# Attention in seven tiles of 128 keys for two pairs of heads, instead of eight tiles of 112

## The chip, the cores and the metric

The kernel runs on one core of a Trainium2 chip. The metric is the device time of one execution in microseconds (us); the kernel before takes 1037.21 us (median of three runs, 1036.66 to 1038.28). A core has a matrix engine (TensorE, in the profile PE for its matmuls and PEld for the loading of their stationary operand), a vector engine (VectorE, DVE), an activation engine (ScalarE, ACT), GpSimd (POOL) and SyncE (SP, which here only starts DMA transfers). Each engine works through its own instructions in order; semaphores tie them together. TensorE writes to PSUM, which the kernel uses as four slots of 128 partitions by two banks of 512 floats.

## The reference

Three stages follow each other: an attention with a sigmoid in place of a softmax, a mixture of experts in which each token goes to one of eight experts, and a gated feed-forward layer.

```
B, H, S, HD = 4, 12, 448, 64                       # attention: q, k, v are (B, H, S, HD)
scores = q @ k.T / sqrt(HD) - log(S)
x = (sigmoid(scores) @ v)  -> (B * S, H * HD) = (1792, 768)
logits = normalised(x) @ normalised(expert_emb).T / tau ; e = argmax(logits) ; gate = softmax(logits)[e]
x = gate * (relu(x @ w1[e]) @ w2[e])               # w1: 768 x 1024, w2: 1024 x 768, 8 experts
out = (sigmoid(x @ w_gate) * (x @ w_val)) @ w_out  # 768 x 1536, 1536 x 768
```

The change is in the attention, and in the small pieces of the routing that run between its steps.

## The kernel before

The 48 heads are 24 pairs (`NP`). A pair fills 128 partitions, one head in partitions 0 to 63, the other in 64 to 127 (`kq`: the pair's keys, 448 columns, then its queries, 448 columns). The 448 keys are cut into `NCH` = 4 tiles of `CP` = 112. One tile of one pair is a unit, with three parts:

- `qk_unit` (L349 to L359): the transposed scores, 112 keys by 448 queries for either head, into one PSUM slot (a bank for each head). Keys and queries are split into a rounded part `hi` and a remainder `lo` (`split_pair`, L341: two VectorE instructions for a pair), and three matmuls hi·hi, hi·lo, lo·hi are summed (L358). The two heads stand in different halves of the array's rows. One ScalarE instruction (L359) then applies the sigmoid to both heads, 112 x 896 elements, into `attn`.
- `av_unit` (L361 to L369): `attn` times the values, in full float32, so that the profile shows two TensorE instructions for each matmul (L364). The contraction is over the tile's 112 keys. The two heads fill different halves of the array's columns. The four tiles of a pair are summed in one PSUM slot `av`; after the last, VectorE copies it to `xT` (L368).
- `logits_unit` (L373): the finished pair's part of the expert logits (L378), in the free bank of the next pair's `av` slot.

The step loop (L834 to L912) sets the order on all engines: it is written out by hand, and each engine's queue follows it. Step `g` makes the scores of units 2g and 2g+1, then the values of the two units before them. 48 steps do the 96 units, and one more step the last values. Other work is put between the steps by their number: `split_pair` two pairs ahead; `load_pair` (three buffers, refilled when a pair has been split) and `load_v` (four buffers) on SP's queue; the decoding of nine packed weight tiles on VectorE (`DEC_AT` says in which steps it begins; three instructions in three steps); after each batch of six pairs the turning of `xT` into rows (`rows_unit`, L402, six transposes on TensorE, a copy on ScalarE, a store to `xd` in DRAM by POOL's queue).

`G0` = 38 is the step after the third of the four batches; `q` counts from there. At `q` = 0 `choose` finds each token's expert (VectorE), at 2 `count` counts the tokens of each expert (TensorE, L477 to L482), then come `fullest`, `ranks` and others (VectorE), at 6 `first_ids` (TensorE, L552) and `gather(0)`, which fetches 128 token rows from `xd` by an indirect DMA on POOL's queue (L794), and at 8 `front(0)`, which transposes the fetched rows (L803). The last four `rows_unit` of the three batches stand at `q` = 0 to 3, so the last rows are stored to `xd` before `gather(0)` reads them.

Of the kernel before, what the change touches and what calls it, by code (L numbers as in the profile page):

```python
# [10 lines left out]
F32 = mybir.dt.float32  # L11
# [15 lines left out]
P = 128  # L27
CP = 112
NCH = S // CP
NPR = H // 2  # L30
NT = N // CP
NTC = N // P
# [18 lines left out]
NDEC = KF2 + NWO  # L51
DEC_ATT = 9
DEC_LEAD = 3
DEC_AT = (4, 8, 13, 17, 22, 26, 31, 36, 42)
DEC_MOE = 2

PZ = 10
# [48 lines left out]
def routed_kernel(ctx: ExitStack, tc: tile.TileContext, kqP, vP, emb, tau, w1P, w2P, wffP, cst, out):  # L106
# [11 lines left out]
    def slot(name):  # L118
        return psp.tile([P, 2, 512], F32, tag="ps", name=name)
# [149 lines left out]

    def load_pair(i):  # L270

        t = ap2.tile([P, 2 * S], F32, tag="kq", name=f"kq{i}", bufs=3)
        SP.dma_start(t, kqP[divmod(i, NPR)])
        kq_t[i] = t

    def load_v(i):
        v = ap2.tile([CP, NCH, P], F32, tag="v", name=f"v{i}", bufs=4)
        SP.dma_start(v.rearrange("p c d -> p (c d)"), vP[divmod(i, NPR)])
        v_t[i] = v

    tau_sb = cpool.tile([P, 1], F32, name="tau_sb")
    emb_sb = ap2.tile([E, D], F32, tag="xr", name="emb_sb", bufs=3)
# [25 lines left out]
    def prepare_constants():  # L308
        V.reciprocal(tau_sb, tau_sb)
        V.tensor_copy(upper_h, C("upper", CP))  # L310
        V.tensor_copy(iota_h, C("iota"))
        V.tensor_copy(ids_h, C("ids", CP))
        V.memset(ones_h, 1.0)
        G.memset(en, 0.0)
        sq = ap1.tile([E, D], BF16, tag="junk", name="sq")
        ssq = cpool.tile([E, 1], F32, name="ssq")
        A.activation(sq, emb_sb, AF.Square, accum_out=ssq)
        rt = cpool.tile([E, 1], F32, name="rt")
        G.tensor_tensor(out=rt, in0=ssq, in1=half_s[:E], op=ALU.pow)
# [17 lines left out]
    ss = cpool.tile([CP, NT], F32, name="ss")  # L337
    ssp = cpool.tile([CP, NCH, 3], F32, name="ssp")
    xT, split_t, attn_t, pav_t = {}, {}, {}, {}

    def split_pair(i):  # L341

        t = kq_t.pop(i)
# [5 lines left out]
    def qk_unit(i, c):  # L349

        hi, lo = split_t[i]
        at_ = ap2.tile([CP, 2, S], F32, tag="attn", name=f"attn{i}_{c}", bufs=6)
        attn_t[i, c] = at_
        ps = slot(f"sc{i}_{c}")
        for a, (k, q) in enumerate(((hi, hi), (hi, lo), (lo, hi))):
            for j in range(2):
                own = slice(j * HD, (j + 1) * HD)
                T.matmul(ps[:CP, j, :S], k[own, c * CP : (c + 1) * CP], q[own, S:], start=(a == 0), stop=(a == 2))  # L358
        A.activation(at_, ps[:CP, :, :S], AF.Sigmoid, bias=bias_s[:CP], scale=1.0 / math.sqrt(HD))  # L359

    def av_unit(i, c):  # L361
        v = v_t[i]
        for j in range(2):
            T.matmul(pav_t[i][j * HD : (j + 1) * HD, 0, :S], v[:, c, j * HD : (j + 1) * HD],  # L364
                     attn_t[i, c][:, j, :], start=(c == 0), stop=(c == NCH - 1))
        if c == NCH - 1:
            x = ap2.tile([P, S], F32, tag="xT", name=f"xT{i}", bufs=8)
            V.tensor_copy(x, pav_t.pop(i)[:, 0, :S])  # L368
            xT[i] = x  # L369
# [46 lines left out]
    def rows_part(part, c):  # L416

        t = TE + c
        k0, n = ((0, 3), (3, 2))[part]
        ps = slot(f"xr{t}_{part}")  # L420
        pv = ps[:CP, 0, : n * P]
        for k in range(n):
            T.transpose(pv[:, k * P : (k + 1) * P], xT[TE // NCH * NPR + k0 + k][:, c * CP : (c + 1) * CP], ident)
        x = ap2.tile([CP, D], F32, tag="xr", name=f"xr_sb{t}_{part}", bufs=3)[:, : n * P]
        A.copy(x, pv)
        (SP if part else G).dma_start(xd[t * CP : (t + 1) * CP, k0 * P : (k0 + n) * P], x)
        later = lambda: square(x, ssp[:, c, part : part + 1], f"{t}_{part}")
        if part and c >= 2:
            squares.append(later)
        else:  # L430
            later()
# [392 lines left out]
    SP.dma_start(emb_sb, emb)  # L824
    load_pair(2)
    load_v(1)
    load_v(2)
    AHEAD = 2
    for n in range(AHEAD):
        split_pair(n)  # L830
        load_pair(n + 3)

    G0 = 2 * NPR * (B - 1) + 2
    for g in range(2 * NP + 1):  # L834
        i, hh = divmod(g, 2)
        if i < NP:
            qk_unit(i, 2 * hh)
            qk_unit(i, 2 * hh + 1)
        if g == 2:
            prepare_constants()  # L840
        elif g == 3:
            prepare_directions()
        elif g == 4:
            prepare_experts()
        q = g - G0
        if g == 2 * NP:
            split_next(eng=G, hi_eng=V)
        ia, ha = divmod(g - 1, 2)
        if q == 2:
            count(0, TE)  # L850
        elif q == 6:
            first_ids(0, TE)
            gather(0)
        elif q == 8:
            front(0)
        if hh == 1 and i + AHEAD < NP:
            split_pair(i + AHEAD)
            if i + AHEAD + 3 < NP:
                load_pair(i + AHEAD + 3)
        if g >= 1:  # L860
            if ha == 0:
                pav_t[ia] = slot(f"av{ia}")
                if ia:
                    logits_unit(ia - 1)
            for c in range(2):
                av_unit(ia, 2 * ha + c)
            if ha == 0 and ia:
                logits_sum(ia - 1)
# [6 lines left out]
        if hh == 1 and i + 3 < NP:  # L875
            load_v(i + 3)
        b, c = divmod(g - 2 * NPR - 2, 2 * NPR)
        if 0 <= b < B - 1:
            if c == 0:
                logits_turn(b)  # L880
            if c < NCH:
                rows_unit(b, c)
        c = g - 2 * (NP - 3) - 2
        if 0 <= c < NCH:
            rows_part(0, c)
        if g >= 2 * NP - 1:
            for c in range(2):
                rows_part(1, 2 * (g - 2 * NP + 1) + c)
        if g == 2 * NP:
            logits_turn(B - 1)  # L890
        if q == 0:
            choose(0, TE)
            RED(out=ohf, in_=oh[:, :TE].rearrange("p t e -> p e t"), axis=AX.X, op=ALU.add)
            V.tensor_copy(ohs, ohf)
            V.tensor_copy(oh4, bct(ohf, NCH))
        elif q == 2:
            fullest()
            expert[0] = SP.value_load(es["tile"], min_val=0, max_val=E - 1)
            ranks(0, TE)
            fullest_ids(0, TE)  # L900
            first_tiles(0, TE)
        elif q == 3:
            columns(0, TE // 2)
        elif q == 4:
            columns(TE // 2, TE)
        if 4 <= q < 4 + NW1:
            load(order.index(("w1", 0, q - 4)))
        if q == 7:
            for k in (0, 1):
                load(order.index(("w2", 0, k)))  # L910
        if q in (6, 7, 8):
            split_next(hi_eng=V if q == 7 else None)  # L912

    hp_t = {}

# [496 lines left out]
```

## Time and profile before

| what | value |
|---|---|
| device time, median of three | 1037.21 us |
| the profiled execution's own time | 1037.45 us |
| its span, first to last instruction | 1035.6 us |
| TensorE busy, matmuls | 1006.4 us, 97% of the span |
| VectorE, ScalarE, GpSimd busy | 58%, 49%, 13% |
| mean granted TensorE clock | 0.99 |
| attention: first score to last value matmul | 4.9 us to about 175 us |

The attention is the first sixth of the span. In the page's 40 slices of 25.9 us each it is the first seven. A busy share is an average: what a change in one stage is worth is read from that stage's own rows. Matmuls are pipelined, so the start of one to the start of the next on the same part of the array tells their cost; the length of one alone holds the time that its last column needs to come out.

### The profile page before, as it was taken

The page shows a single profiled execution, that of the slowest core. Times are in us where ns is not written, and L with a number is a line of the kernel's source. Part 1 is how long each engine was busy: PE and PEld are TensorE (multiplying, and loading weights), DVE is VectorE, ACT ScalarE, POOL GpSimd, SP SyncE. Part 2 cuts the span into 40 slices and gives each one's busy share as a digit, 9 for nine tenths or more (in the row PEclk, how much of TensorE's full clock was granted, in tenths as well). Part 3 has the DMA queues.
Part 4 walks back from the last instruction along what each step waited for, and adds up shares of the span by engine and source line. Part 5 has one row for each costly group of instructions (what it writes and reads, how often), then busy time and mean ns, then how long its engine had stood idle before and what let it go on. Part 6 is the DMA issues. An engine that isn't in the chain of part 4 may idle for free.

```text
span 1035.6 us, 15304 instructions
## 1 busy us (share of the span) xinstructions
PE 1006.4 (97%) x6144; PEld 822.7 (79%) x6144; DVE 597.2 (58%) x660; ACT 503.1 (49%) x546; POOL 138.4 (13%) x109
## 2 busy tenths in 40 slices
PE   9999999878999999999999999999999999999996
PEld 4455455676887788888888899888899888899995
DVE  5665577986887877787658743334332333323551
ACT  5576678536766676777502432233322333323540
POOL 0010012643242122111100000200000000001001
PEclk9999999989999999999999999999999999999998
DMA  7878786112689876765458652422333333324630
GB/s 254 303 257 300 247 304 231 71 32 110 247 265 415 289 263 269 253 221 211 166 169 280 236 180 99 143 99 92 122 122 123 125 108 103 122 92 143 196 119 31
DMA packets 38526, 191.94 MB, mean 185 GB/s; under 512 B 4952, under 2 KB 5992, under 8 KB 36016
## 3 DMA queue, kind: packets, MB, share of 16 engines
q1 hardware_dynamic: 30560, 152.84, 43.3%
q0 software_dynamic: 7888, 38.05, 9.8%
q8 instruction: 50, 0.82, 0.3%
q14 instruction: 28, 0.23, 0.1%
HBM read 197.46 MB, written 31.16 MB: 221 GB/s over the span
## 4 chain that ended last, share of the span: by engine, by line
PE 73%; DVE 0%; issue 0%; DMA 0%; POOLq 0%; ACT 0%
PE gv L1154 11%; PE gv L1153 11%; PE gv L1155 11%; PE h L935 8%; PE o L921 5%; PE o L919 5%; PE o L920 5%; PE y L919 3%; PE y L921 3%; PE y L920 3%; PE qh L1024 1%; PE qy L1047 1%; PE hTp L954 1%; PE yTp L1139 1%; PE xTp L803 1%
## 5 line engine op out<-in xcount | busy, mean ns | idle before, releaser
L213 DVE TENSOR_TENSOR lo<-rawb,hi 128x1536 fp32r<-128x1536 f32 x173 | 302.1, 1756 | 289.9 <-ACT hi L212 286.3
L212 ACT CAST hi<-rawb 128x1536 fp32r<-128x1536 f32 x178 | 262.8, 1480 | 244.7 <-PE gv L1154 96.3
L1153 PE MATMUL gv<-yT,hi 128*128 128x512 f32 (+1 forms) x576 | 208.9, 363 | 0.0
L1155 PE MATMUL gv<-yT,lo 128*128 128x512 f32 (+1 forms) x576 | 208.9, 363 | 0.0
L1154 PE MATMUL gv<-yT,hi 128*128 128x512 f32 (+1 forms) x576 | 208.8, 363 | 0.0
L1155 PEld LDWEIGHTS gv<-yT,lo 128*128 128x128 f32 x576 | 108.7, 189 | 16.9
L1153 PEld LDWEIGHTS gv<-yT,hi 128*128 128x128 f32 x576 | 108.7, 189 | 16.8
L1154 PEld LDWEIGHTS gv<-yT,hi 128*128 128x128 f32 x576 | 108.7, 189 | 16.7
L919 PE MATMUL o<-hi,gh 128*128 128x384 f32 x336 | 112.8, 336 | 0.0
L921 PE MATMUL o<-lo,gh 128*128 128x384 f32 x336 | 112.3, 334 | 0.0
L920 PE MATMUL o<-hi,gl 128*128 128x384 f32 x336 | 112.3, 334 | 0.0
L359 ACT ACTIVATE attn<-sc,bias_s 112x896 f32<-112x896 f32 x96 | 91.2, 1001 | 41.9 <-PE sc L358 41.9
L1324 ACT CAST gh<-sg 128x512 fp32r<-128x512 f32 (+1 forms) x48 | 27.2, 567 | 132.1 <-DVE sg L1323 132.1
L364 PE MATMUL av<-attn,v 112*64 112x448 f32 x384 | 82.8, 552 | 0.0
L919 PE MATMUL y<-hi,hh 128*128 128x384 f32 x208 | 72.7, 349 | 0.0
L935 PE MATMUL h<-hi,xh 128*128 128x512 f32 x168 | 69.2, 412 | 3.5 <-PEq L1078 3.4
L935 PE MATMUL h<-lo,xh 128*128 128x512 f32 x168 | 67.1, 399 | 4.5 <-DVE lo L213 4.5
L921 PE MATMUL y<-lo,hh 128*128 128x384 f32 x208 | 70.5, 339 | 0.3 <-DVE lo L213 0.3
L920 PE MATMUL y<-hi,hl 128*128 128x384 f32 x208 | 70.3, 338 | 0.0
L1343 POOL DMA_INDIRECT out<-ob,idc x13 | 17.8, 1373 | 370.5 <-DVE ob L1372 340.1
L920 PEld LDWEIGHTS o<-hi,gl 128*128 128x128 f32 x336 | 63.1, 188 | 0.1
L919 PEld LDWEIGHTS o<-hi,gh 128*128 128x128 f32 x336 | 63.1, 188 | 0.1
(302 smaller groups left out, 1311.9 us busy)
## 6 DMA issues: line engine op xcount, KB each, us to landing
rawb<-wd SPq DMA_DIRECT2D x65, 768.0 KB
rawb<-in_w1P SPq DMA_DIRECT2D x52, 768.0 KB
rawb<-in_w2P SPq DMA_DIRECT2D x52, 768.0 KB
rawb<-in_wffP SPq DMA_DIRECT2D x16, 1536.0 KB
wd<-rawb POOLq DMA_DIRECT2D x16, 768.0 KB, 7.9
kq<-in_kqP SPq DMA_DIRECT2D x24, 448.0 KB
v<-in_vP SPq DMA_DIRECT2D x24, 224.0 KB
xd<-xr_sb POOLq DMA_DIRECT2D x12, 336.0 KB, 5.2
```

What stands on the lines that cost most here:

```text
L212: (hi_eng.tensor_copy if hi_eng else A.copy)(hi, raw)
L213: eng.tensor_sub(lo, raw, hi)
L359: A.activation(at_, ps[:CP, :, :S], AF.Sigmoid, bias=bias_s[:CP], scale=1.0 / math.sqrt(HD))
L364: T.matmul(pav_t[i][j * HD : (j + 1) * HD, 0, :S], v[:, c, j * HD : (j + 1) * HD], attn_t[i, c][:, j, :], start=(c == 0), stop=(c == NCH - 1))
L919: T.matmul(o, ah[:, ks], bh[:, w], start=(k == 0), stop=False)
L920: T.matmul(o, al[:, ks], bh[:, w], start=False, stop=False)
L921: T.matmul(o, ah[:, ks], bl[:, w], start=False, stop=(k == nk - 1))
L935: T.matmul(ps[:, half, :], x[:, k * P : (k + 1) * P], w[:, s * 512 : (s + 1) * 512], start=(k == 0 and x is xh and w is hi), stop=(k == KD ...
L1153: T.matmul(o, hi[:, a, k, :], yh[:, k, :n], start=(k == 0), stop=False)
L1154: T.matmul(o, hi[:, a, k, :], yl[:, k, :n], start=False, stop=False)
L1155: T.matmul(o, lo[:, a, k, :], yh[:, k, :n], start=False, stop=(k == KD - 1))
L1324: A.copy(gh[:, f, :n], sg[:, :n])
```

## The change

Two pairs of heads now share seven tiles of 128 keys (`NU` = 7). Of each pair, keys 0 to 383 are three whole tiles. The last 64 keys of both pairs make the joint tile, number 3 of the seven: pair 2d in rows 0 to 63, pair 2d+1 in rows 64 to 127. 12 doubles of pairs by 7 make 84 units in 42 steps. In the joint unit `qk_unit` does one float32 matmul for each head and pair, straight from `kq` without the split, and `av_unit` four matmuls of 64 rows by 64 columns, into the `av` slots of both pairs. So `kq` has to stay until the joint unit has read it (five buffers instead of three), and is loaded two pairs at a time after the joint unit; the values of two pairs are one load of 448 KB (two buffers), laid out on the host. The pieces of the routing and of the decoding get new step numbers, and `G0` becomes 33.

```diff
+NU = 2 * S // P
+KQ = 5
-DEC_AT = (4, 8, 13, 17, 22, 26, 31, 36, 42)
+DEC_AT = (3, 7, 11, 15, 19, 23, 27, 31, 36)
     def load_pair(i):
-        t = ap2.tile([P, 2 * S], F32, tag="kq", name=f"kq{i}", bufs=3)
+        t = ap2.tile([P, 2 * S], F32, tag="kq", name=f"kq{i}", bufs=KQ)
-    def load_v(i):
-        v = ap2.tile([CP, NCH, P], F32, tag="v", name=f"v{i}", bufs=4)
+    def load_v(d):
+        v = ap2.tile([P, NU, P], F32, tag="v", name=f"v{d}", bufs=2)
...
+    def parts_of(u):
+        d, n = divmod(u, NU)
+        if n == NU // 2:
+            return [(2 * d + p, S - HD, slice(p * HD, (p + 1) * HD)) for p in range(2)]
+        return [(2 * d + n // 4, n % 4 * P, slice(0, P))]
+    def qk_unit(u):
+        at_ = ap2.tile([P, 2, S], F32, tag="attn", name=f"attn{u}", bufs=6)
+        attn_t[u] = at_
+        ps = slot(f"sc{u}")
+        both = len(parts_of(u)) == 2
+        for a in range(1 if both else 3):
             for j in range(2):
                 own = slice(j * HD, (j + 1) * HD)
-                T.matmul(ps[:CP, j, :S], k[own, c * CP : (c + 1) * CP], q[own, S:], start=(a == 0), stop=(a == 2))
-        A.activation(at_, ps[:CP, :, :S], AF.Sigmoid, bias=bias_s[:CP], scale=1.0 / math.sqrt(HD))
+                for i, k0, rows in parts_of(u):
+                    hi, lo = (kq_t[i],) * 2 if both else split_t[i]
+                    k, q = ((hi, hi), (hi, lo), (lo, hi))[a]
+                    T.matmul(ps[rows, j, :S], k[own, k0 : k0 + rows.stop - rows.start], q[own, S:],
+                             start=(a == 0), stop=(both or a == 2))
+        A.activation(at_, ps[:, :, :S], AF.Sigmoid, bias=bias_s, scale=1.0 / math.sqrt(HD))
+    def first_unit(i):
+        return i // 2 * NU + i % 2 * (NU // 2)
+    def last_unit(i):
+        return first_unit(i) + NU // 2
+    def av_unit(u):
+        av_open(u)
+        v, at_ = v_t[u // NU], attn_t.pop(u)
         for j in range(2):
+            for i, _, rows in parts_of(u):
+                T.matmul(pav_t[i][j * HD : (j + 1) * HD, 0, :S], v[rows, u % NU, j * HD : (j + 1) * HD],
+                         at_[rows, j, :], start=(u == first_unit(i)), stop=(u == last_unit(i)))
...
-    G0 = 2 * NPR * (B - 1) + 2
-    for g in range(2 * NP + 1):
+    NS = NP // 2 * NU // 2
+    LG = [(last_unit((b + 1) * NPR - 1) + 1) // 2 + 2 for b in range(B - 1)]
+    G0 = LG[-1]
+    for g in range(NS + 1):
...
-        if q == 2:
+        if q == 1:
             count(0, TE)
-        elif q == 6:
+        elif q == 4:
             first_ids(0, TE)
             gather(0)
-        elif q == 8:
+        elif q == 6:
             front(0)
...
+        for n in range(2, NP):
+            if max(0, (first_unit(n) - 6) // 2) == g:
+                split_pair(n)
...
+                if u % NU == NU // 2:
+                    for n in range(u // NU * 2, u // NU * 2 + 2):
+                        if n + KQ < NP:
+                            load_pair(n + KQ)
+                if u % NU == NU - 1 and u // NU + 2 < NP // 2:
+                    load_v(u // NU + 2)
...
-        elif q == 2:
+        elif q == 1:
             fullest()
...
+        elif q == 2:
+            columns(0, TE // 2)
         elif q == 3:
-            columns(0, TE // 2)
-        elif q == 4:
             columns(TE // 2, TE)
```

`logits_turn` and `rows_unit` of batch b now begin in step `LG[b]`, which is 12, 23 and 33 (before: 14, 26 and 38).

Three places show how the order moves. The first is TensorE's queue at one step of the attention. Before, pair 3's second and third tile follow each other with pair 2's last values between them (`sc` is a unit's score slot, `av` a pair's value slot, and `x2` stands for the two heads):

```order
L358 MATMUL sc3_1_413<-kqhi3_312 112x448 x2
L358 MATMUL sc3_1_413<-kqlo3_313,kqhi3_312 112x448 x2
L358 MATMUL sc3_1_413<-kqhi3_312,kqlo3_313 112x448 x2
L364 MATMUL av2_384<-attn2_2_360,v2_186 64x448 x2
L364 MATMUL av2_384<-attn2_3_369,v2_186 64x448 x2
L358 MATMUL sc3_2_430<-kqhi3_312 112x448 x2
L358 MATMUL sc3_2_430<-kqlo3_313,kqhi3_312 112x448 x2
L358 MATMUL sc3_2_430<-kqhi3_312,kqlo3_313 112x448 x2
```

In the changed kernel the joint unit of pairs 2 and 3 is unit 10. Its scores are made in step 5:

```order
L375 MATMUL sc10_364<-kq2_182 64x448
L375 MATMUL sc10_364<-kq3_194 64x448
L375 MATMUL sc10_364<-kq2_182 64x448
L375 MATMUL sc10_364<-kq3_194 64x448
L375 MATMUL sc11_371<-kqhi3_280 128x448 x2
L375 MATMUL sc11_371<-kqlo3_281,kqhi3_280 128x448 x2
L375 MATMUL sc11_371<-kqhi3_280,kqlo3_281 128x448 x2
```

and its values in step 6, ahead of those of unit 11:

```order
L395 MATMUL av2_356<-attn10_363,v1_184 64x448
L395 MATMUL av3_417<-attn10_363,v1_184 64x448
L395 MATMUL av2_356<-attn10_363,v1_184 64x448
L395 MATMUL av3_417<-attn10_363,v1_184 64x448
L395 MATMUL av3_417<-attn11_370,v1_184 64x448 x2
```

Six rows of a whole unit's scores became four of 64 keys each, and a joint unit stands either first or last in its step's scores and in its step's values.

The second place is TensorE's queue ahead of `first_ids` (`ps0_0`, from `bm`). Before, whole steps lie between the last rows of the third batch (`xr11`) and it; right ahead of it stand the values of pair 21 and the scores of pair 22:

```order
L364 MATMUL av21_1781<-attn21_0_1732,v21_1499 64x448 x2
L364 MATMUL av21_1781<-attn21_1_1741,v21_1499 64x448 x2
L358 MATMUL sc22_0_1794<-kqhi22_1703 112x448 x2
L358 MATMUL sc22_0_1794<-kqlo22_1704,kqhi22_1703 112x448 x2
L358 MATMUL sc22_0_1794<-kqhi22_1703,kqlo22_1704 112x448 x2
L358 MATMUL sc22_1_1803<-kqhi22_1703 112x448 x2
L358 MATMUL sc22_1_1803<-kqlo22_1704,kqhi22_1703 112x448 x2
L358 MATMUL sc22_1_1803<-kqhi22_1703,kqlo22_1704 112x448 x2
L552 LDWEIGHTS bm_130
```

In the changed kernel the last rows stand one step's scores ahead of it:

```order
L440 MATMUL xr11_1585<-cs_92,xT17_1354 112x128
L375 MATMUL sc74_1600<-kqhi21_1378 128x448 x2
L375 MATMUL sc74_1600<-kqlo21_1379,kqhi21_1378 128x448 x2
L375 MATMUL sc74_1600<-kqhi21_1378,kqlo21_1379 128x448 x2
L375 MATMUL sc75_1609<-kqhi21_1378 128x448 x2
L375 MATMUL sc75_1609<-kqlo21_1379,kqhi21_1378 128x448 x2
L375 MATMUL sc75_1609<-kqhi21_1378,kqlo21_1379 128x448 x2
L584 LDWEIGHTS bm_130
```

`first_ids` and with it the gather moved up in the queue, close behind the rows that the gather's source needs: one step's scores lie between them, where three steps' scores and two steps' values lay.

The third place is SP's queue in the first third of the attention. Before, one pair and one pair's values take turns, with a packed weight tile (`rawb` from `wffP`) now and then:

```order
L273 DMA kq8_451<-in_kqP 128x896
L278 DMA v6_463<-in_vP 112x512
L273 DMA kq9_512<-in_kqP 128x896
L278 DMA v7_525<-in_vP 112x512
L188 DMA rawb_91<-in_wffP 128x3072
L273 DMA kq10_576<-in_kqP 128x896
```

In the changed kernel two pairs come together, then the values of two pairs:

```order
L275 DMA kq7_426<-in_kqP 128x896
L275 DMA kq8_428<-in_kqP 128x896
L281 DMA v3_463<-in_vP 128x896
L190 DMA rawb_91<-in_wffP 128x3072
L275 DMA kq9_525<-in_kqP 128x896
L275 DMA kq10_527<-in_kqP 128x896
L281 DMA v4_587<-in_vP 128x896
L190 DMA rawb_91<-in_wffP 128x3072
```

The bytes are nearly the same; a pair's buffer is now freed by the joint unit and no longer by the split.

## Rows read from the trace of the kernel before

**Rows 1.** Windows: span, then engines' busy us (instructions), clock, DMA share, GB/s

```profile
40.00:60.00 20.00, 20.00 (x155) 10.15 (x151) 12.98 (x17) 13.63 (x17) 2.18 (x4) 1.00 0.86 302
180.00:200.00 20.00, 14.85 (x78) 11.52 (x77) 17.52 (x42) 11.04 (x15) 10.97 (x4) 0.91 0.30 99
```

**Rows 2.** Timeline of PE, a plain step: start, length, line, op, tiles, shape, count

```profile
71.43 0.55 PE L364 MATMUL av<-attn,v 112*64 112x448 f32 x2
71.90 0.46 PE L358 MATMUL sc<-kqhi 64*112 64x448 f32 x2
72.20 0.36 PE L358 MATMUL sc<-kqlo,kqhi 64*112 64x448 f32 x2
...
73.00 0.37 PE L358 MATMUL sc<-kqhi,kqlo 64*112 64x448 f32 x2
73.30 1.72 PE L364 MATMUL av<-attn,v 112*64 112x448 f32 x8
74.95 0.46 PE L358 MATMUL sc<-kqhi 64*112 64x448 f32 x2
```

**Rows 3.** Timeline of PE, logits, values and rows in a fuller step

```profile
62.67 0.40 PE L378 MATMUL av<-xT,en 128*32 128x112 f32 x8
63.00 1.72 PE L364 MATMUL av<-attn,v 112*64 112x448 f32 x8
64.66 0.87 PE L408 MATMUL xr<-cs,xT 128*112 128x128 f32 x6
65.45 0.46 PE L358 MATMUL sc<-kqhi 64*112 64x448 f32 x2
```

**Rows 4.** Groups by line, window 0 to 330 us: busy, mean ns | idle before

```profile
L359 ACT ACTIVATE attn<-sc,bias_s 112x896 f32<-112x896 f32 x96 | 91.2, 1001 | 41.9 <-PE sc L358 41.9
```

**Rows 5.** Timeline of DVE around the choice of experts

```profile
137.06 1.75 DVE L201 SCALAR_TENSOR_TENSOR rawb<-rawb 128x1536 uint32<-128x1536 uint32 x1
138.73 0.18 DVE L395 COPY lg<-lg 112x32 f32<-112x32 f32 x1
140.11 0.26 DVE L469 TENSOR_TENSOR oh<-eq,m 112x96 f16<-112x96 f32 x1
140.93 0.62 DVE L345 CAST kqhi<-kq 128x896 fp32r<-128x896 f32 x1
141.58 1.09 DVE L346 TENSOR_TENSOR kqlo<-kq,kqhi 128x896 fp32r<-128x896 f32 x1
145.43 0.62 DVE L368 COPY xT<-av 128x448 f32<-128x448 f32 x1 [2.57 <-PE av L364]
```

**Rows 6.** Timeline of POOL and PE around the first gather

```profile
151.50 0.52 POOL L411 DMA_DIRECT2D xd<-xr_sb  x1 [3.66 <-ACT xr_sb L410]
159.70 1.05 POOL L794 DMA_INDIRECT xg<-xd,idx  x1 [7.68 <-DVE idx L553]
...
150.30 0.46 PE L358 MATMUL sc<-kqhi 64*112 64x448 f32 x2
158.18 0.45 PE L552 MATMUL ps<-am,bm 112*128 112x1 f16 x12
158.56 1.72 PE L364 MATMUL av<-attn,v 112*64 112x448 f32 x8
165.96 0.87 PE L803 MATMUL xTp<-cs,xg 128*128 128x128 f32 x6
```

**Rows 7.** By line: L411 from 130 us on, then L794: landing, waits

```profile
DMA to landing us min/median/max: 3.5/5.7/7.0
...
L794 POOLq EVENT_SEMAPHORE  x3: 43/43/43, 158.5 to 158.7; - x3
DMA to landing us min/median/max: 4.0/4.0/4.0
```

**Rows 8.** Waits, window 0 to 176 us: us in total, times, longest

```profile
DVE kqhi L345 <- DMA kq<-in_kqP: 6.6, 2, 3.5
```

**Rows 9.** Timeline of PE after the attention

```profile
194.85 0.60 PE L935 MATMUL h<-lo,xh 128*128 128x512 f32 x1 [4.49 <-DVE lo L213]
```

More of the change, by code (lines that the diff above doesn't have):

```diff
@@ L270, in load_pair @@
     def load_pair(i):
-        t = ap2.tile([P, 2 * S], F32, tag="kq", name=f"kq{i}", bufs=3)
+        t = ap2.tile([P, 2 * S], F32, tag="kq", name=f"kq{i}", bufs=KQ)
         SP.dma_start(t, kqP[divmod(i, NPR)])
         kq_t[i] = t
-    def load_v(i):
-        v = ap2.tile([CP, NCH, P], F32, tag="v", name=f"v{i}", bufs=4)
-        SP.dma_start(v.rearrange("p c d -> p (c d)"), vP[divmod(i, NPR)])
-        v_t[i] = v
+    def load_v(d):
+        v = ap2.tile([P, NU, P], F32, tag="v", name=f"v{d}", bufs=2)
+        SP.dma_start(v.rearrange("p c d -> p (c d)"), vP[d])
+        v_t[d] = v
     tau_sb = cpool.tile([P, 1], F32, name="tau_sb")
@@ L339, in routed_kernel @@
     xT, split_t, attn_t, pav_t = {}, {}, {}, {}
+    summed = set()
     def split_pair(i):
-        t = kq_t.pop(i)
+        t = kq_t[i]
         hi, lo = [ring.tile([P, CH], F32R, tag=g, name=f"kq{g}{i}")[:, : 2 * S] for g in ("hi", "lo")]
@@ L347, in split_pair @@
         split_t[i] = (hi, lo)
[L349 to L355, printed above, removed]
+    def parts_of(u):
[3 more added lines that the diff above has]
+        return [(2 * d + n // 4, n % 4 * P, slice(0, P))]
@@ L361, in av_unit @@
-    def av_unit(i, c):
-        v = v_t[i]
-        for j in range(2):
[L364 to L369, printed above, removed]
+                for i, k0, rows in parts_of(u):
[3 more added lines that the diff above has]
+                             start=(a == 0), stop=(both or a == 2))
@@ new lines, in qk_unit, with av_open @@
+        A.activation(at_, ps[:, :, :S], AF.Sigmoid, bias=bias_s, scale=1.0 / math.sqrt(HD))
[3 more added lines that the diff above has]
+        return first_unit(i) + NU // 2
+    def av_open(u):
+        for i, _, _ in parts_of(u):
+            if u == first_unit(i) and i not in pav_t:
+                pav_t[i] = slot(f"av{i}")
+    def av_unit(u):
+        av_open(u)
+        v, at_ = v_t[u // NU], attn_t.pop(u)
+        for j in range(2):
+            for i, _, rows in parts_of(u):
+                T.matmul(pav_t[i][j * HD : (j + 1) * HD, 0, :S], v[rows, u % NU, j * HD : (j + 1) * HD],
+                         at_[rows, j, :], start=(u == first_unit(i)), stop=(u == last_unit(i)))
+        for i, _, _ in parts_of(u):
+            if u == last_unit(i):
+                x = ap2.tile([P, S], F32, tag="xT", name=f"xT{i}", bufs=8)
+                V.tensor_copy(x, pav_t[i][:, 0, :S])
+                xT[i] = x
@@ L826, in routed_kernel @@
     load_v(1)
-    load_v(2)
-    AHEAD = 2
-    for n in range(AHEAD):
+    for n in range(2):
         split_pair(n)
-        load_pair(n + 3)
-    G0 = 2 * NPR * (B - 1) + 2
-    for g in range(2 * NP + 1):
[L835 to L839, printed above, removed]
+    for n in range(3, KQ):
+        load_pair(n)
+    NS = NP // 2 * NU // 2
+    LG = [(last_unit((b + 1) * NPR - 1) + 1) // 2 + 2 for b in range(B - 1)]
@@ L840, in routed_kernel @@
+    G0 = LG[-1]
+    for g in range(NS + 1):
+        if g < NS:
+            qk_unit(2 * g)
+            qk_unit(2 * g + 1)
+        if g == 1:
             prepare_constants()
+        elif g == 2:
+            prepare_directions()
         elif g == 3:
-            prepare_directions()
-        elif g == 4:
             prepare_experts()
         q = g - G0
-        if g == 2 * NP:
+        if g == NS:
             split_next(eng=G, hi_eng=V)
-        ia, ha = divmod(g - 1, 2)
-        if q == 2:
+        if q == 1:
@@ L850, in routed_kernel @@
             count(0, TE)
-        elif q == 6:
+        elif q == 4:
             first_ids(0, TE)
             gather(0)
-        elif q == 8:
+        elif q == 6:
             front(0)
[L856 to L859, printed above, removed]
+        for n in range(2, NP):
+            if max(0, (first_unit(n) - 6) // 2) == g:
+                split_pair(n)
         if g >= 1:
[L861 to L868, printed above, removed]
+            units = (2 * g - 2, 2 * g - 1)
+            av_open(units[0])
+            ready = [i for i in sorted(xT) if i + 1 in pav_t and i not in summed]
+            for i in ready:
+                logits_unit(i)
+            for u in units:
+                av_unit(u)
+            for i in ready:
+                logits_sum(i)
+                summed.add(i)
+            for u in units:
+                if u % NU == NU // 2:
[4 more added lines that the diff above has]
+                    load_v(u // NU + 2)
@@ L874, in routed_kernel @@
                 decode(DEC_ORDER[k], r)
[L875 to L878, printed above, removed]
+        for b in range(B - 1):
+            c = g - LG[b]
             if c == 0:
                 logits_turn(b)
-            if c < NCH:
+            if 0 <= c < NCH:
                 rows_unit(b, c)
-        c = g - 2 * (NP - 3) - 2
+        c = g - last_unit(NP - 4) // 2 - 2
         if 0 <= c < NCH:
             rows_part(0, c)
-        if g >= 2 * NP - 1:
+        if g >= NS - 1:
             for c in range(2):
-                rows_part(1, 2 * (g - 2 * NP + 1) + c)
-        if g == 2 * NP:
+                rows_part(1, 2 * (g - NS + 1) + c)
+        if g == NS:
             logits_turn(B - 1)
@@ L901, in routed_kernel @@
             first_tiles(0, TE)
+        elif q == 2:
+            columns(0, TE // 2)
         elif q == 3:
-            columns(0, TE // 2)
-        elif q == 4:
             columns(TE // 2, TE)
-        if 4 <= q < 4 + NW1:
-            load(order.index(("w1", 0, q - 4)))
-        if q == 7:
+        if 3 <= q < 3 + NW1:
+            load(order.index(("w1", 0, q - 3)))
+        if q == 6:
             for k in (0, 1):
                 load(order.index(("w2", 0, k)))
-        if q in (6, 7, 8):
-            split_next(hi_eng=V if q == 7 else None)
+        if q in (5, 6, 7):
+            split_next(hi_eng=V if q == 6 else None)
     hp_t = {}
@@ L1389 @@
     kqP = np.concatenate([feat(k), feat(q)], 3)
-    vP = v.reshape(B, NPR, 2, NCH, CP, HD).transpose(0, 1, 4, 3, 2, 5).reshape(B, NPR, CP, NCH * P)
+    vt = v.reshape(-1, 2, 2, S, HD).transpose(0, 1, 3, 2, 4).reshape(-1, 2, S, P)
+    whole = vt[:, :, : S - HD].reshape(-1, 2, S // P, P, P)
+    left = vt[:, :, S - HD :].reshape(-1, 1, P, P)
+    vP = np.concatenate([whole[:, 0], left, whole[:, 1]], 1).transpose(0, 2, 1, 3).reshape(-1, P, NU * P)
     w1P = f["moe_w1"].reshape(E, KD, P, F1).transpose(0, 2, 1, 3).reshape(E, P, KD * F1)
```

## The prediction

> **What bounds the kernel now.** I read the windows first. In a window of the attention TensorE is busy for all 20.00 of 20 us at full clock, while VectorE, ScalarE and the DMA engines have room [rows 1]. The timeline of TensorE says whether that busy time is work or waiting inside a matmul: a plain step repeats every 3.05 us (71.90 to 74.95), its matmuls start at an even pitch, and no releaser stands in its rows [rows 2]. So the step's matmul starts alone set its length, and what the attention gains or loses is a count of pitches. ScalarE's sigmoids wait for TensorE's scores and not the other way round [rows 4], and VectorE's splits waited for a load of keys twice only in 24 pairs, 6.6 us together [rows 8]. Behind the attention TensorE has gaps of its own, 14.85 busy of 20 us [rows 1], which hang on VectorE [rows 9]; they begin with the attention's end and should move with it.
>
> **What a step consists of.** The scores take 1.40 us (71.90 to 73.30). The second matmul starts 0.30 after the first and the last 0.80 later, four pitches of 0.20. So a whole unit is 3 x 0.20 = 0.60, and 0.20 goes once for entering and leaving this shape [rows 2]. The values take 1.65 us. Their eight instructions go two by two; the last two start 0.47 before the next scores (71.43 and 71.90), which leaves 1.18 for three pitches, 0.39 each. A unit is two pitches, 0.78, and about 0.09 goes once. The logits add 0.33 and the six transposes of a row block 0.79 [rows 3]. The tiles' 112 or 128 keys appear nowhere in these pitches: what streams is the 448 queries.
>
> **The change part by part.**
>
> *Six steps less.* 48 steps become 42, with the same logits, rows, counts and splits in all. 6 x 3.05 = 18.3 us go. The stationary tile of a whole unit grows from 112 to 128 columns. Its load lies beside the matmul before it. If it no longer fitted there, the pitch could grow in proportion at the most, 0.20 to 0.23, 3 x 0.03 x 72 units = 6 us; at the least it costs nothing. I take nothing, since the pitch is already what 448 columns need at 2.4 GHz (0.187) and a small remainder. A sigmoid on 128 rows instead of 112 has the same 896 elements in a row, so 84 of them at 1.00 us replace 96 [rows 4]: 12 us of ScalarE that nobody waited for, worth nothing.
>
> *The joint unit's scores.* Four float32 matmuls in quarters of the array, two instructions each. No row here has this shape. The nearest are the values: two halves of the array side by side at 0.39 a pitch [rows 2], and the logits, where four quarters of the columns put eight instructions into 0.33 [rows 3]. If four quarters run side by side as these do, the unit is two pitches, 0.78, and 0.09 for the change of shape. The whole unit beside it in the same step is 0.60 + 0.20. Together 1.67 against 1.40: 0.27 more in each of 12 steps, or 3.2 us.
>
> *The joint unit's values.* Two pitches like any unit, and one more change of shape, 0.09 to 0.15: I take 0.12, 1.5 us for 12. Scores and values together cost 4.7 us. Bounds for both: if entering a new shape were free, 12 x 0.18 = 2.2; if two of the quarters had to wait for the other two, 0.78 more at each place, which is the first rival.
>
> The Trainium skill has a rule that speaks against this part: "TensorEngine Tiling", section "Key Properties", says that changing the tiling mode, and not merely the tile, drains TensorE. The trace agrees in kind, with 0.1 to 0.2 us at each change between scores and values [rows 2]. With the fixed latency of about 166 ns that "TensorE: Matmul & The Clock Gate" gives in "Single matmul latency", the 24 additional changes would be an estimated 4.0 us and the two joint parts 12 x 0.18 + 4.0 = 6.2 instead of 4.7.
>
> *The count, one step sooner.* `count` now follows the choice of experts by one step's scores. On VectorE, counted from the start of step 33: the third batch's last values end 0.87 before it, then come the copy to `xT` (0.62), a decoding (1.75), a split (140.93 to 142.67, 1.74), the logits' sum (like the 0.26 of a small operation), a decoding (1.75), and from there to the end of `oh` 1.56 (138.81 to 140.37) [rows 5]. That is 6.8 us. TensorE arrives there after 1.67 + 0.33 + 1.65 + 0.1 for one transpose + 0.79 + 1.40 = 6.0 us. It waits 0.8 us; before, a further step lay between and it did not wait. Behind it the joint values of unit 66 are queued and everything after them.
>
> *The gather, two steps sooner.* POOL's gather stands behind the landing of the last rows in `xd`. Before: the rows' transposes end at 150.30, the store starts 1.20 later [rows 6], POOL's queue is let go at 158.5 (7.0 us of landing, the longest of four, median 5.7, shortest 3.5), the gather's 4.0 us end at 163.7 [rows 7], and the transposes at 165.96 find the rows there [rows 6]. After: counted from the same transposes' end, the gather is let go at 1.2 + 5.7 + 0.3 and has landed at 11.2 us (9.0 to 12.5 with the other two landings). TensorE arrives at `front(0)` after one step with `first_ids` and joint values, 1.40 + 0.38 + 1.77, one step with logits and half a row block, 1.40 + 0.33 + 1.65 + 0.4, and the scores of a third, 1.40: 8.7 us. It waits 2.5 us (0.3 to 3.8). Queued behind `front(0)` are the values and so the whole step.
>
> *Loads, decoding, start.* The same bytes in other portions. Keys of an odd pair now have four steps (12 us and more) from the freeing of their buffer to their split, where they had six; this is hidden as long as the DMA engines keep their pace, see the third rival. The first load of values is 224 KB larger: at 302 GB/s [rows 1] 0.7 us if the first values waited for it; I take nothing, since the scores of four units are made first. The decodings keep their number and their three instructions of at most 1.75 us.
>
> *Sum.* -18.3 + 4.7 + 0.8 + 2.5 = -10.3 us. The profiled execution's own time is 1037.45 (span 1035.6 and 1.85 around it), 0.24 above the median of the runs. 1037.45 - 10.3 = 1027.1. With the rest of the kernel unchanged, that is the forecast.
>
> **The rivals.**
>
> 1. The quarters do not run four at a time. In the joint unit two pairs of heads stream four different operands into the two halves of the rows, and no row shows more than two halves of rows or four quarters of columns at once. With two at a time each joint part takes 0.78 more: 12 x 2 x 0.78 = 18.7, and the time is 1045.8, slower than before. The point from which it decides is 10.3 / 24 = 0.43 us for each joint part. For it speaks that the shape is new; against it, that halves of rows (scores) and of columns (values) each run side by side in rows 2 without loss. The Trainium skill's "TensorEngine Tiling" lists 64 by 64 in "Available Configurations" as four independent tiles; no run here shows it yet.
> 2. Only one of the two joint parts is slowed so, scores or values: 9.4 us more, 1036.5, no change that can be told.
> 3. Keys or values come too late in every double of pairs, because they are asked for later and in larger portions. At half a microsecond of TensorE's time for each of 12 doubles it is 6 us, 1033.1. For it: the DMA share is 0.86 at 302 GB/s [rows 1] and all of it must now pass in less time. Against it: in 12 us at that rate 3.6 MB pass, and a double needs two pairs and its values, 1.3 MB, and on the average three quarters of a packed tile and its store, 1.8 MB.
> 4. Neither of the two new waits appears, since VectorE or the store's landing is quicker than I count: -13.6, 1023.9.
>
> A further danger within the forecast is the clock. The one long stop behind the attention, 4.49 us [rows 9], lies in the window whose granted clock is 0.91 [rows 1]. A wait of 3.8 us at `front(0)` could cost the clock for some microseconds, some 2 us more.
>
> **How the numbers follow.** Forecast 0.60, with a range of its own from 1024 to 1031 (the landing's bounds, the changes of shape, half of the wider pitch). Rival 1 0.12, rival 2 0.07, rival 3 0.08, rival 4 0.13. A change under 0.2% (2.1 us) can't be told from none. Faster: forecast, rivals 3 and 4, 0.81. Within 0.2%: rival 2, 0.07. Slower: rival 1, 0.12. The range for 8 in 10 reaches down to the fourth rival and up past the third, 1022 to 1035; rivals 1 and 2 are left out.
>
> **What would show it.** In the profile after: 84 sigmoids of about 1.00 us; plain steps still 3.05 long; the joint scores as two bursts of four instructions 0.39 apart and the next shape some 0.5 behind the second; joint values the same; a wait of 0.8 us of the count's first matmul for VectorE's `oh`; a wait of about 2.5 us of `xTp` for the DMA into `xg`; the last value matmul ending at about 165 us instead of 175, and the gaps behind it as long as before. Wrong it would be if the joint bursts are four of two instructions (rival 1 or 2), if whole units' matmuls start more than 0.20 apart, if VectorE's splits wait for `kq` in the middle of the attention (rival 3), or if the stop behind the attention grows by what the attention gave up.

## The result, and the profile after

The changed kernel takes 1041.99 us (median of six runs, 1041.26 to 1048.81), the kernel before, run beside it, 1036.81. The ratio is 1.0064 with an interval of 1.0037 to 1.0091: slower, where 1027.1 was forecast. The profiled execution took 1045.53 us with a span of 1043.7; it is 3.5 us above the median of the six. The lines below say that the tiles did nearly what was forecast, and that TensorE stood still where the routing was moved up.

The timeline of TensorE, kernel after, around the first joint units (columns as in [rows 2]):

```profile
20.09 0.47 PE L375 MATMUL sc<-kqhi 64*128 64x448 f32 x2
...
23.16 0.98 PE L375 MATMUL sc<-kq 64*64 64x448 f32 x8
24.07 0.47 PE L375 MATMUL sc<-kqhi 64*128 64x448 f32 x2
...
24.87 0.59 PE L410 MATMUL av<-xT,en 128*32 128x112 f32 x16
...
28.47 1.89 PE L395 MATMUL av<-attn,v 64*64 64x448 f32 x12
30.29 0.47 PE L375 MATMUL sc<-kqhi 64*128 64x448 f32 x2
```

A plain step is 3.07 us (20.09 to 23.16), where [rows 2] have 3.05. The joint unit's eight score instructions take 0.91 us to the start of the next shape (23.16 to 24.07), the whole unit behind it 0.80; together 1.71 where a plain step has 1.40. The values with a joint unit take 1.82 (28.47 to 30.29) where a plain step has 1.65. The sigmoids answer to [rows 4], in the groups by line:

```profile
L377 ACT ACTIVATE attn<-sc,bias_s 128x896 f32<-128x896 f32 x84 | 79.9, 1001 | 41.2 <-PE sc L375 41.1
```

The same timeline at the three places where TensorE waits long or where a wait was forecast:

```profile
17.98 0.53 PE L333 MATMUL pe__315<-cs,emb_sb 8*128 8x8 f32 x6 [2.31 <-DVE xT L400]
...
133.39 0.20 PE L509 MATMUL pk<-oh,upper_h 112*112 112x96 f16 x1 [0.48 <-DVE oh L501]
...
163.19 1.52 PE L835 MATMUL xTp<-cs,xg 128*128 128x128 f32 x6 [8.36 <-DMA xg<-xd,idx]
164.64 3.14 PE L395 MATMUL av<-attn,v 128*64 128x448 f32 x8
167.71 0.54 PE L455 MATMUL xr<-cs,xT 128*112 128x128 f32 x3
168.81 0.98 PE L375 MATMUL sc<-kq 64*64 64x448 f32 x8 [0.57 <-ACT xr_sb L457]
...
178.77 1.72 PE L395 MATMUL av<-attn,v 128*64 128x448 f32 x8
```

The last value matmul ends at 180.5 us, not at 165. The largest stop is `front(0)`'s wait for the gathered rows, 8.36 us; behind it transposes and values take 1.5 and 3.1 us where they take 0.8 and 1.7 in other steps. The windows say why (columns as in [rows 1]):

```profile
150.00:160.00 10.00, 4.84 (x41) 2.53 (x37) 5.56 (x5) 6.17 (x8) 2.20 (x3) 0.86 0.73 267
160.00:170.00 10.00, 6.24 (x27) 2.70 (x29) 4.12 (x4) 2.03 (x5) 0.53 (x1) 0.62 0.45 159
180.00:200.00 20.00, 14.43 (x99) 10.95 (x96) 16.91 (x50) 12.39 (x24) 10.30 (x4) 0.96 0.40 135
```

The granted clock is 0.86 and then 0.62: behind the stop TensorE runs for a while at the lower of its two levels, 1.2 GHz. POOL's and SP's timelines show when the gather could go out, and beside what. POOL, after, answering to [rows 6]:

```profile
146.94 0.53 POOL L443 DMA_DIRECT2D xd<-xr_sb  x1 [3.97 <-ACT xr_sb L442]
155.57 1.05 POOL L826 DMA_INDIRECT xg<-xd,idx  x1 [8.11 <-DVE rawb L203]
```

The gather's line in full, answering to [rows 7], has these two rows, when POOL's queue was let go and how long the gather took to land:

```profile
L826 POOLq EVENT_SEMAPHORE  x3: 42/43/43, 154.6 to 154.7; - x3
...
DMA to landing us min/median/max: 7.5/7.5/7.5
```

SP's queue, after, and then before:

```profile
154.95 0.86 SPq L172 DMA_DIRECT2D rawb<-in_w2P  x2
```

```profile
162.65 0.87 SPq L170 DMA_DIRECT2D rawb<-in_w2P  x2
```

The store was issued at 146.94 and landed 7.6 us later, when POOL's queue was let go (154.6), and the gather went out at 155.57 and landed 7.5 us later, not 4.0. The gather's row names a decoding on VectorE (`rawb`) as what came last, but that did not hold it: from the release of POOL's queue to the gather it is 1.0 us in the changed kernel and in all seven runs below, while that decoding ended anywhere from 0.65 us ahead of the gather to its very start. Two loads of `w2`, 768 KB each, were issued from 154.95 on, just ahead of it. Before, the same loads went out at 162.65, 2.95 us behind the gather.

### The profile page after: what moved, and what is told of

Read it like the earlier page. It is cut to its first block, busy times and chain, and to the rows that moved or that the text cites. A ratio compares the mean times of both kernels' runs of the same rounds, so it can differ in the third digit from the quotient of the medians.

```text
span 1043.7 us, 15196 instructions
## 1 busy us (share of the span) xinstructions
PE 1001.3 (96%) x6096; PEld 815.0 (78%) x6096; DVE 597.0 (57%) x660; ACT 492.4 (47%) x534; POOL 135.4 (13%) x109
## 4 chain that ended last, share of the span: by engine, by line
PE 72%; DMA 2%; issue 1%; DVE 0%; POOLq 0%; ACT 0%; ACTq 0%
PE gv L1194 11%; PE gv L1192 11%; PE gv L1193 11%; PE h L974 8%; PE o L960 5%; PE o L958 5%; PE o L959 5%; PE y L958 3%; PE y L960 3%; PE y L959 3%; PE qh L1063 1%; PE qy L1086 1%; PE hTp L993 1%; DMA xg<-xd,idx 1%; PE yTp L1178 1%
## 5 line engine op out<-in xcount | busy, mean ns | idle before, releaser
L377 ACT ACTIVATE attn<-sc,bias_s 128x896 f32<-128x896 f32 x84 | 79.9, 1001 | 41.2 <-PE sc L375 41.1
L395 PE MATMUL av<-attn,v 128*64 128x448 f32 (+1 forms) x384 | 75.9, 564 | 0.0
L960 PEld LDWEIGHTS o<-lo,gh 128*128 128x128 f32 x336 | 63.1, 188 | 0.0
```

Of the source, the lines that this page charges most:

```text
L377: A.activation(at_, ps[:, :, :S], AF.Sigmoid, bias=bias_s, scale=1.0 / math.sqrt(HD))
L395: T.matmul(pav_t[i][j * HD : (j + 1) * HD, 0, :S], v[rows, u % NU, j * HD : (j + 1) * HD], at_[rows, j, :], start=(u == first_unit(i)), st ...
L960: T.matmul(o, ah[:, ks], bl[:, w], start=False, stop=(k == nk - 1))
```

## The experiments

Theory A: the tiles gain what was forecast, and the time is lost at stops of TensorE that the new step numbers made, above all at `front(0)`. A1 is a part of it: the loads of `w2` ahead of the gather slow it. Theory B, the rival: the new tiles themselves cost the time, in a slower pace or behind the attention.

**`front(0)` two steps later.**

```diff
-        elif q == 6:
+        elif q == 8:
             front(0)
```

> The changed kernel with front(0), the transposes of the first gathered rows, at q = 8 instead of 6; the gather itself stays at q = 4. Theory A (the tiles gain what was forecast, and the stop of TensorE at front(0) with the slow clock behind it eats it): the wait of xTp for xg, 8.4 us, is gone, step 39 takes about 4.3 instead of 15.5 us, and the time is about 1031 us. Theory B (the loss is in the new tiles or behind the attention, and the stop only shows it): another wait takes its place and the time stays within 2 us of 1042.

Measured: 1033.12 us (ten runs, 1031.93 to 1035.52), ratio to before 0.9955 (0.9938 to 0.9973). This one number turns a kernel that is slower than before into a faster one, 8.9 us below the changed kernel; step 39 takes 4.5 us. Theory A holds, 2 us short of its figure. TensorE's timeline:

```profile
163.14 0.87 PE L835 MATMUL xTp<-cs,xg 128*128 128x128 f32 x6
163.94 0.96 PE L395 MATMUL av<-attn,v 64*64 64x448 f32 x2
165.27 1.88 PE L395 MATMUL av<-attn,v 64*64 64x448 f32 x10 [0.36 <-ACT attn L377]
...
169.18 1.72 PE L395 MATMUL av<-attn,v 128*64 128x448 f32 x8
```

No wait stands at the transposes, the clock is 1.00 from 150 to 180 us, and the last value matmul ends at 170.9. The gather still took 7.7 us; it is hidden now. New small waits for ScalarE's `attn`, 0.35 to 0.41 us each, appear in the last steps.

**The two loads of `w2` two steps later, `front(0)` left where the change put it.**

```diff
-        if q == 6:
+        if q == 8:
             for k in (0, 1):
                 load(order.index(("w2", 0, k)))
```

> The changed kernel with the two loads of w2 emitted at q = 8 instead of 6, behind the first stores of rows on SP's queue, so that they start after the gather. Theory A1 (the gather landed late because 1.5 MB of w2 were ahead of it on the DMA engines): its landing falls from 7.5 to about 4 us, the wait at front(0) from 8.4 to about 5, the time to about 1037 to 1039 us. Theory A2 (the gather itself is slow, or only the store of the last rows decides): the landing stays at 7 us or more and the time at 1042.

Measured: 1038.35 us (ten runs, 1035.73 to 1041.68), ratio 1.0004 (0.9983 to 1.0026). The gather's line:

```profile
  PE xTp L835: 4.8, 1
...
DMA to landing us min/median/max: 4.2/4.2/4.2
```

The landing is back at 4.2 us, the wait down from 8.4 to 4.8. A1 holds, and the remaining 4.8 us are the chain of store, landing and gather without the loads.

**The experts' transposes (`prepare_experts`) one step later.**

```diff
-        elif g == 3:
+        elif g == 4:
             prepare_experts()
```

> The changed kernel with prepare_experts in step 4 instead of 3. If the wait of pe_ for VectorE's xT (2.3 us, the step 5.9 long) is a loss of its own, it goes, and the time falls by about 2.5 us to 1039.5. If the later stop at front(0) swallows it, because that stop ends with a transfer whose time is set elsewhere, the time stays at 1042: not expected, since the transfer starts from the attention's own rows.

Measured: 1040.29 us (ten runs, 1039.2 to 1045.18), ratio 1.0039 (1.0019 to 1.0059). That is 1.7 less than the changed kernel, too close to its scatter to be read from the times alone. The trace shows the wait smaller and at another instruction:

```profile
15.47 1.72 PE L395 MATMUL av<-attn,v 128*64 128x448 f32 x8
17.87 0.47 PE L375 MATMUL sc<-kqhi 64*128 64x448 f32 x2 [0.68 <-DVE xT L400]
...
19.29 0.54 PE L333 MATMUL pe__338<-cs,emb_sb 8*128 8x8 f32 x6
```

The stop is 0.68 instead of 2.31 us: whoever comes first to the PSUM slot that pair 0's values held has to wait until VectorE has copied them out. Last value matmul at 179.4.

**The kernel before, with the routing alone moved up** (the old tiles, old transposes and loads):

```diff
-        if q == 2:
+        if q == 1:
             count(0, TE)
-        elif q == 6:
+        elif q == 4:
             first_ids(0, TE)
             gather(0)
-        elif q == 8:
+        elif q == 6:
             front(0)
```

and `fullest` and what follows it one step earlier, `columns` in steps 2 and 3.

> The kernel before, with 112-key tiles, and of the change only the routing moved up: count and fullest at q = 1, columns at 2 and 3, first_ids and gather(0) at 4, front(0) at 6. Theory A: the store of the last rows still lands at about 158.5 us and the gather 4 to 5 us later, while TensorE comes to front(0) at about 158.2: it waits some 5 us, with a clock loss of 0 to 3 behind it, and the time is 1042 to 1046 us. Theory B (moving the routing costs nothing by itself): 1037 us.

Measured: 1047.66 us (four runs, 1047.58 to 1048.11), ratio 1.0093 (1.0056 to 1.013): 10.8 us slower than before without one new tile. That refutes this run's theory B. It is more than expected. The last value matmul ends 10.9 us later than in the kernel before (186.3 and 175.4), so all of it is lost in the attention, and the timeline shows where:

```profile
140.43 0.25 PE L477 MATMUL pk<-oh,upper_h 112*112 112x96 f16 x1 [1.62 <-DVE oh L469]
...
141.50 3.01 PE L364 MATMUL av<-attn,v 112*64 112x448 f32 x8
144.44 1.22 PE L408 MATMUL xr<-cs,xT 128*112 128x128 f32 x6
...
166.84 1.51 PE L803 MATMUL xTp<-cs,xg 128*128 128x128 f32 x6 [4.54 <-DMA xg<-xd,idx]
168.29 3.26 PE L364 MATMUL av<-attn,v 112*64 112x448 f32 x8
```

Two waits, 1.62 at the count and 4.54 at `front(0)`, are 6.2 us. The other 4.6 fit what stands behind each of them: values of 3.0 and 3.3 us instead of 1.65, with a granted clock of 0.83 from 140 to 150 us and 0.78 from 160 to 170:

```profile
140.00:150.00 10.00, 9.47 (x63) 4.73 (x65) 6.93 (x31) 4.62 (x8) 0.75 (x2) 0.83 0.53 202
160.00:170.00 10.00, 5.46 (x30) 2.95 (x28) 3.41 (x4) 2.95 (x4) 1.05 (x1) 0.78 0.24 85
```

The gather itself took 3.8 us here, with the `w2` loads behind it.

**The wait filled.** In the changed kernel 38 matmuls of zeros, which nothing uses, ahead of `front(0)`'s transposes, so that TensorE is busy while the gather is under way:

```diff
         psf = ps.rearrange("p a b -> p (a b)")
+        if p == 0:
+            for i in range(38):
+                T.matmul(ps[:, i % 2, :], wz[:, :P], wz, start=True, stop=True)
```

> Changed kernel with 38 additional matmuls of zeros (512 columns, bf16, into front(0)'s own PSUM slot) ahead of the transposes of front(0), so that TensorE is busy through the wait for the gather (some 8 us at full clock). They compute nothing that is used. Theory (the clock granted after the stop costs some 2.8 us on top of the wait): the granted clock stays at 1.0 from 150 to 170 us, step 39 is 12.5 us long instead of 15.5, time 1042.0 - 2.8 = 1039.2 us. Rival (the step is long because of its wait alone, or the clock falls for another reason): time 1042 us, clock still under 0.9 in 160 to 170 us.

Measured: 1040.97 us (twelve runs, 1038.9 to 1043.03), ratio 1.0033 (1.002 to 1.0047): one us below the changed kernel, and the two intervals overlap, so the time alone settles nothing. Its timeline and window do for this place:

```profile
157.66 8.38 PE L836 MATMUL xTp<-wz 128*128 128x512 bf16 x38
167.09 0.88 PE L838 MATMUL xTp<-cs,xg 128*128 128x128 f32 x6 [1.06 <-DMA xg<-xd,idx]
167.90 1.72 PE L395 MATMUL av<-attn,v 128*64 128x448 f32 x8
169.55 0.54 PE L455 MATMUL xr<-cs,xT 128*112 128x128 f32 x3
170.03 0.98 PE L375 MATMUL sc<-kq 64*64 64x448 f32 x8
```

```profile
160.00:170.00 10.00, 8.94 (x45) 3.97 (x43) 1.80 (x3) 1.45 (x2) 0.53 (x1) 1.00 0.75 273
```

At a clock of 1.00 the way from the first transpose to the next step's scores is 2.94 us (167.09 to 170.03); behind the unfilled wait it was 5.62 (163.19 to 168.81). The clock and what hangs on it, ScalarE's late copy among it, cost 2.7 us. Step 39 took 13.8 us, where 12.5 was expected and 15.5 had been measured: the gather took 8.7 us to land in this run, 1.2 more than in the changed kernel's profile.

**Two steps later for `front(0)` and one for the experts, together.**

```diff
-        elif g == 3:
+        elif g == 4:
             prepare_experts()
...
-        elif q == 6:
+        elif q == 8:
             front(0)
```

> Changed kernel with front(0) two steps later and the experts' transposes (pe_) one step later. Theory (the two stops are separate terms of TensorE's queue and add up): the last value matmul ends at about 169 us (170.9 with the later front alone, 1.7 less for the experts), the time is 1033.1 - 1.7 = 1031.4 us. Rival (what is freed early is lost again, because the chain store, landing, gather moves up with the attention and the last step hangs on ScalarE): the last step gets longer by the same, time 1033, as with the later front alone.

Measured: 1032.21 us (eight runs, 1030.28 to 1035.75), ratio 0.9953 (0.9933 to 0.9972). The last value matmul ends at 169.2, where theory A had it, but 1031.4 and the rival's 1033 lie within the runs' scatter: inconclusive by the time.

**All three: experts one step later, `front(0)` one step later (`q` 7), `w2` two steps later (`q` 8).**

```diff
-        elif g == 3:
+        elif g == 4:
             prepare_experts()
...
-        elif q == 6:
+        elif q == 7:
             front(0)
...
-        if q == 6:
+        if q == 8:
             for k in (0, 1):
                 load(order.index(("w2", 0, k)))
```

> Changed kernel with the experts' transposes one step later, front(0) one step later (between the old place and that of the run with the later front) and the two w2 loads two steps later. Theory: with the loads behind it the gather lands in some 4 us, so that front(0) finds its rows one step later with no wait or at most 0.5 us, and the last step, which is then free of front's transposes and casts, is some 2 us shorter than with front(0) two steps later: last value matmul at 166 to 168 us, time 1029 to 1030 us. Rival (landing of the gather is governed by other traffic, or the store lands later): front(0) waits 2 us or more, time 1032 us or more.

Measured: 1029.77 us (six runs, 1028.13 to 1030.63), ratio 0.9923 (0.9903 to 0.9944). This beats both kernels. Only step numbers differ from the changed kernel, so theory B, that the new tiles themselves cost the time, is refuted.

```profile
157.83 0.85 PE L835 MATMUL xTp<-cs,xg 128*128 128x128 f32 x6 [0.42 <-DMA xg<-xd,idx]
158.60 0.40 PE L410 MATMUL av<-xT,en 128*32 128x112 f32 x8
...
166.83 1.72 PE L395 MATMUL av<-attn,v 128*64 128x448 f32 x8
```

The gather landed in 4.5 us, `front(0)` waits 0.42, and the last values end at 168.5, a little later than the 166 to 168 expected; waits of 0.2 to 0.4 us for ScalarE and VectorE stand in the last three steps.

## Why the prediction was wrong, point by point

The step that failed is **"The gather, two steps sooner"**: 2.5 us (0.3 to 3.8) were put down, 8.36 were measured, and the clock behind it took 2.7 more. With 10.3 us saved the attention would have ended at 165.1; it ended at 180.5, and of these 15.4 us the step and its clock are 8.6. Its parts, counted from the end of the last rows' transposes (145.73, the start of the next scores):

| part | forecast, us | measured, us |
|---|---|---|
| transposes' end to store | 1.2 | 1.2 (146.94) |
| store to POOL let go | 5.7, the median landing | 7.6 (154.6) |
| let go to gather issued | 0.3 | 1.0 (155.57) |
| gather issued to landed | 4.0 | 7.5 (163.1) |
| TensorE's arrival | 8.7 | 9.1 (154.8) |

Two of these could have been had from the rows. The last store of the batch had the longest landing, 7.0 [rows 7], and it is the last store that counts. POOL's queue was let go at 158.5 and the gather stood at 159.70 [rows 6, 7], 1.2 us and not 0.3. That stretch held a wait of its own, since the gather also needs the token numbers (`idx`) from VectorE. Their rows, before and after:

```profile
159.27 0.15 DVE L553 CAST idx<-ps 128x1 int32<-128x1 f32 x1
```

```profile
147.63 0.16 DVE L585 CAST idx<-ps 128x1 int32<-128x1 f32 x1 [0.57 <-PE ps L584]
```

Before, they were ready only at 159.42, behind a decoding; the 0.3 is about what lies between them and the gather. After, they were ready almost 7 us before the store had landed, and the 1.0 us from the release to the gather is left. With 7.0, 1.2 and 4.0 the sum is 13.4 - 8.7 = 4.7 us, and the run with the later `w2` loads measured 4.8. That it is so close is partly luck: the parts there were 7.4, 1.0 and 4.2, and TensorE came after 9.1. The other 3.5 us the prediction did not see: it carried the gather's 4.0 us over as they were, and did not ask which loads would now come ahead of it. SP's loads of `w2` were issued 2.95 us behind the gather before and 0.6 ahead of it after. The runs tell it apart: with the loads behind the gather it took 3.8, 4.2 and 4.5 us to land, with the loads ahead 7.5 to 8.7 in five. The Trainium skill says in "DMA: Bandwidth & Descriptors", section "Issuing engines are not separate DMA queues", that transfers started by ScalarE, SyncE or GpSimd run on the same 16 DMA engines and interleave. The landings agree: 4.2 us against 7.5 when only the loads on SP's queue were moved. What makes the last store take 7 us or more, where another took 3.5 [rows 7], was not tested.

The "further danger within the forecast", the clock, was right in kind: some 2 us for a wait of 3.8 were named outside the sum, 2.7 us came behind a wait of 8.36.

**What the sum did not have.** The experts' transposes at the start wait 2.31 us for VectorE's copy of pair 0's values. VectorE's timeline of the start, before:

```profile
13.40 0.56 DVE L368 COPY xT<-av 128x448 f32<-128x448 f32 x1
14.46 0.14 DVE L299 TENSOR_SCALAR rt<-rt 8x1 f32<-8x1 f32 x1 [0.49 <-POOL rt L319]
...
17.32 1.09 DVE L346 TENSOR_TENSOR kqlo<-kq,kqhi 128x896 fp32r<-128x896 f32 x1
```

and after:

```profile
13.43 0.14 DVE L302 TENSOR_SCALAR rt<-rt 8x1 f32<-8x1 f32 x1
...
16.29 1.09 DVE L350 TENSOR_TENSOR kqlo<-kq,kqhi 128x896 fp32r<-128x896 f32 x1
17.30 0.62 DVE L400 COPY xT<-av 128x448 f32<-128x448 f32 x1
```

The copy stood ahead of a chain of small operations and a split and now stands behind them. The sum priced the start at nothing because four units' scores come ahead of the first values; the PSUM slots were not looked at. The logits' turning (`lg`) waits 0.37 us for VectorE at two places, and the first and the last step are 0.5 and 1.0 us longer than before. No run isolates these last three.

**Six steps less** held. The pitch stayed at 0.20 and the plain step at 3.07. With an estimated 0.5 us for the 0.02 more in each plain step the saving is 17.8 of 18.3.

**The joint unit** held in its mechanism: 0.31 more for the scores, 0.17 for the values, 12 x 0.48 = 5.8 us for the 4.7 forecast. Rival 1 needed 0.78 more at each place, rival 2 at one; both are refuted by 0.91 us for a whole burst of eight scores and 1.82 us for the values of a joint and a whole unit. The prediction's other figure for the two joint parts, 6.2 us, was nearer than its 4.7. "TensorEngine Tiling (Array Packing)" in the Trainium skill lists 64 by 64 under "Available Configurations" as four tiles. This trace now shows four at a time: the eight instructions take 0.91 us.

**The count**: 0.48 measured for 0.8 forecast. Both sides of it came later than forecast, counted from the start of step 33 (126.03): `oh` after 7.3 us instead of 6.8, TensorE after 6.9 instead of 6.0. **Rival 3** is refuted: VectorE's `kqhi` waited for keys 6.6 us, twice, as in [rows 8]. **Rival 4** failed, since both waits came.

The terms come near the trace: -17.8 + 5.8 + 0.5 (count) + 8.4 + 2.7 (`front(0)`) + 2.3 (experts) + 0.8 (`lg`) + 1.5 (first and last step) = +4.2, and the last value matmul moved by +5.1 (175.4 to 180.5). So 0.9 us are not accounted for; two gaps of 0.45 us instead of 0.20 in the scores of steps 34 and 35 are half of that. The +5.1 is also what lies between the medians (5.2). Behind the attention the profiled run took 863.2 us against 860.2. Over the profiled runs of the experiments that stretch was 857.5 to 863.8 with no order by edit, and what sets it was not followed.

With the stops shortened by three step numbers the time is 1029.77, 2.7 above the forecast and within the range given for it. That is no proof of the sum: the forecast held 2.5 us for the wait at `front(0)`, which is 0.42 in that run, so by its own terms 1025.0 would have been due. The terms that the sum had too low or not at all (the joint unit, the pace of the steps, the experts, `lg`, the first and the last step) are together of the size of the 4.8 us between.

## What to carry to other kernels

When work is packed into fewer steps, everything that is placed by step number comes closer together in time; a transfer that two steps used to hide may not fit in the new two. So price a moved chain by the row of the very instruction that ends it (the last store's landing, not the median), from each queue's release to its next issue, and list which other transfers change places with it in time. A stop of TensorE can cost twice, once as the wait (8.36 us here) and once more as the lower clock behind it (2.7), and the cure may be to move the reader by one step and a bulk load behind it.

## What the runs showed of the hardware that had not been expected

Four quarters of the array, 64 rows by 64 columns each with its own operands, did eight float32 instructions of 448 columns in 0.91 us, change of shape included.

An indirect gather that took 3.8 to 4.5 us to land took 7.5 to 8.7 with 1.5 MB of loads from another queue ahead of it. From the release of POOL's queue by the store's landing to the gather it was 1.0 us each time, except before, where `idx` was late.

A wait of only 1.62 us was followed by a granted clock of 0.83 from 140 to 150 us in the run with the old tiles. The 2.31 us at the experts' transposes left the clock at 1.00 in the changed kernel's profile, and 2.46 us at the same place in the run with `front(0)` two steps later did so too. In the profile of the run with the filled wait, whose program is the same at the start, that stop was 2.76 us, and its row and the windows read:

```profile
17.89 0.80 PE L333 MATMUL pe__315<-cs,emb_sb 8*128 8x8 f32 x6 [2.76 <-DVE xT L400]
```

```profile
0.00:20.00 20.00, 15.18 (x89) 7.18 (x91) 11.28 (x28) 9.59 (x11) 2.95 (x8) 0.94 0.80 304
20.00:40.00 20.00, 20.00 (x146) 8.62 (x142) 11.23 (x14) 9.71 (x10) 0.76 (x1) 0.89 0.59 225
```

So a stop at the same place may or may not cost the clock in a given execution, and a shorter stop (1.62) was followed by the lower clock where a longer one (2.46) was not. That this makes the changed kernel's spread (1041 to 1049) wider than that of the version without long stops (1028 to 1031) is a guess that no run isolated.
